# Weight decoding in five VectorE steps with range totals, spread over the first batch, more banks for early scratch, and a reordered prologue

## The chip, the core and the metric

The kernel runs on one core of a Trainium2 chip. The metric is the device time of one execution in microseconds (us). The engines of the core that matter here are TensorE (PE; its weight loads are listed apart as PEld), VectorE (DVE), ScalarE (ACT), GpSimd (POOL) and the queue that issues most transfers (SP). Each engine works through its own queue in order. What the measurement of this kernel can tell from no change is about 0.3%, some 4 us.

## The reference

Attention over clusters, and behind it a feed-forward block. For each of 4 batches and 8 heads there are 768 queries, keys and values of 64 numbers, and 16 centroids per head. Every query and key goes to the centroid whose direction is nearest, and a query sees only keys of its own cluster:

```
mask = q_assign[:, :, :, None] == k_assign[:, :, None, :]
scores = np.where(mask, scale * q @ k.T, -1e9)
attn = softmax(scores);  x = attn @ v      # (B*S, 512)
h = x @ w_in                               # 512 -> 2048
out = (h * clip(h + 3, 0, 6) / 6) @ w_out  # 2048 -> 512
```

The weights `w_in` and `w_out` arrive as 64-bit floats, 16.8 MB in all, and the engines cannot compute with these: they are loaded as pairs of 32-bit words (`lo`, `hi`) and decoded to 32-bit floats on the chip.

## The kernel before

`fast_path` does everything unless an input is out of range; a flag `ok` at the end chooses whether `general_path` is run afterwards (it never is here).

**Attention.** Heads are taken in 16 pairs, and a pair has 12 steps: 2 halves of the queries (`HALF` = 384) by 6 blocks of keys. A step (`scores`, then `attn_v` two steps later) is: TensorE makes the scores `ps`, ScalarE their exponent `ex` (L304), GpSimd adds `ex` to a running sum `acc` (L308 for the first sum of a half, L311 for the other four, five sums in each half), TensorE multiplies with the values (`pv`). Four steps after a half has ended `divide` sums `acc` over partitions on TensorE (`pd`, L342), and VectorE takes the reciprocal `rcp` (L346) and writes the quotient to `xT` (L347). The reciprocals are the clearest marks of progress in the trace: one per half, 8 in each batch of 4 pairs, 32 in all. I call the time from one reciprocal to the next "a half".

**Preparation of a pair.** While a pair runs, the next one is prepared: four groups of transposes (`turn`, tile `pqk`, copied to `xf` by VectorE and ScalarE in turn), the match with the centroids (`route`: `pr` on TensorE, then six VectorE instructions L248 to L264 up to the one-hot `oh`), and three groups of matmuls that turn `oh` round (`route_turn`, `po` to `xm`). All of these and `pd` share one PSUM buffer, the pool `psum_t` with one slot: the next group cannot be written before the copy of the last one has ended.

**Weights.** 32 chunks of 128x512 numbers, 16 of `w_in`, then 16 of `w_out`, 512 KB each. `load_weights` needs one of two `raw` buffers; `decode_chunk` has eight steps in a chain across two engines: VectorE cuts out exponent (L57) and fraction (L61), GpSimd clamps and shifts the exponent (L64, L67) and scales the fraction (L70), VectorE adds the low word (L73), multiplies (L76) and sets the sign (L77). By the source, 8 chunks are decoded in every 15 steps.

**Feed-forward.** When batch b has gone through `divide`, its feed-forward items go into a list `fill` and are put between the steps of batch b+1: `up` (`ph`, L368; ScalarE `t`, L375; VectorE `gT`, L377) and `down` (`py`, L390). They have the two slots of `psum_m`. While batch 0 runs there is nothing in `fill` and `psum_m` is empty. So the program has a first stage (prologue and batch 0, attention and decoding), a long second stage (three batches of attention with feed-forward work between), and the feed-forward work of the last batch by itself.

**What sets the order.** Within an engine the order is not the source's: a scheduler of the framework places each instruction by its own model of when its inputs and its buffer are ready. The queues as built are what counts, and the section on the change shows pieces of them.

**Range checks.** `divide` also folds `pd <= BOUND` into a tile `good` on VectorE (L352) and adds `rcp` to `inverses` on GpSimd (L355); at the end these give `ok`.

## Time and profile before

| what | value |
|---|---|
| device time, median of 3 runs | 1276.08 us (1273.18 to 1277.16) |
| the profiled execution | 1276.86 us |
| its span in the trace | 1274.5 us |
| busy: PE, DVE, POOL, ACT | 94%, 34%, 32%, 21% of the span |
| first `ex` starts | 30.88 us |
| first, seventh, eighth reciprocal start | 71.6, 216.0, 239.0 us |
| PE busy from 239 to 1122 us | 883.0 of 883.0 us |
| last copy of `y` starts | 1266.6 us |

The busy shares are means over stages that differ. Read by stretches, VectorE and GpSimd work most of the time up to some 240 us and little after it, TensorE has idle time up to there and none after it. The clock column (PEclk) gives the granted clock of TensorE as a share of the full 2.4 GHz.

### The profile page before, as it was taken

The page shows a single profiled execution, that of the slowest core. Times are in us where ns is not written, and L with a number is a line of the kernel's source. Part 1 is how long each engine was busy: PE and PEld are TensorE (multiplying, and loading weights), DVE is VectorE, ACT ScalarE, POOL GpSimd, SP SyncE. Part 2 cuts the span into 40 slices and gives each one's busy share as a digit, 9 for nine tenths or more (in the row PEclk, how much of TensorE's full clock was granted, in tenths as well). Part 3 has the DMA queues.
Part 4 walks back from the last instruction along what each step waited for, and adds up shares of the span by engine and source line. Part 5 has one row for each costly group of instructions (what it writes and reads, how often), then busy time and mean ns, then how long its engine had stood idle before and what let it go on. Part 6 is the DMA issues. An engine that isn't in the chain of part 4 may idle for free.

```text
span 1274.5 us, 11438 instructions
## 1 busy us (share of the span) xinstructions
PE 1196.9 (94%) x4610; PEld 546.9 (43%) x4610; DVE 439.0 (34%) x588; ACT 270.3 (21%) x403; POOL 409.5 (32%) x315
## 2 busy tenths in 40 slices
PE   5767777899999999999999999999999999999997
PEld 3323323445444454454434454454434444554553
DVE  5888778733213221232221322232212222120110
ACT  1222222232212320223112231123211321020110
POOL 2778677633232321233222322233322332000000
PEclk9788878799999999999999999999999999999999
DMA  5322332301010100201011010110110000000000
GB/s 141 91 85 85 103 91 79 104 1 38 5 46 12 25 13 9 54 1 38 1 30 33 13 25 9 29 25 15 23 30 9 1 1 8 17 1 16 9 9 20
DMA packets 83646, 42.81 MB, mean 34 GB/s; under 512 B 76416, under 2 KB 76416, under 8 KB 83584
## 3 DMA queue, kind: packets, MB, share of 16 engines
q1 hardware_dynamic: 83328, 41.95, 12.1%
q8 instruction: 38, 0.62, 0.2%
q14 instruction: 24, 0.20, 0.0%
q10 hardware_dynamic: 256, 0.03, 0.0%
HBM read 35.68 MB, written 6.29 MB: 33 GB/s over the span
## 4 chain that ended last, share of the span: by engine, by line
PE 82%; DVE 8%; POOL 6%; issue 2%; DMA 1%; ACTq 0%; ACT 0%; POOLq 0%
PE ph L368 27%; PE py L390 27%; PE ps L300 12%; PE pv L321 9%; DVE wfr L76 3%; PE pr L242 3%; POOL acc L311 2%; PE pqk L228 2%; POOL wex L64 1%; PE pd L342 1%; POOL wfr L70 1%; POOL wex L67 1%; PE po L276 1%; DVE wfr L73 1%; DVE rcp L346 1%
## 5 line engine op out<-in xcount | busy, mean ns | idle before, releaser
L368 PE MATMUL ph<-xT,w_in_sb 128*128 128x384 f32 x1024 | 359.3, 501 | 0.0
L311 POOL TENSOR_TENSOR acc<-acc,ex 128x768 f32<-128x768 f32 x128 | 241.0, 1883 | 327.5 <-ACT ex L304 325.9
L390 PE MATMUL py<-w_out_sb,gT 128*128 128x512 f32 x768 | 345.8, 602 | 0.0
L304 ACT ACTIVATE ex<-ps 128x768 f32<-128x768 f32 x192 | 155.7, 811 | 463.9 <-PE ps L300 455.4
L368 PEld LDWEIGHTS ph<-xT,w_in_sb 128*128 128x128 f32 x1024 | 190.9, 193 | 146.9 <-issue 25.3
L390 PEld LDWEIGHTS py<-w_out_sb,gT 128*128 128x128 f32 x768 | 142.8, 191 | 176.4 <-issue 175.8
L300 PE MATMUL ps<-xf 64*128 64x384 f32 x768 | 201.1, 569 | 0.0
L377 DVE SCALAR_TENSOR_TENSOR gT<-t,ph 128x384 f32<-128x384 f32 x128 | 70.8, 553 | 328.4 <-ACT t L375 328.3
L321 PE MATMUL pv<-ex,vt 128*64 128x384 f32 x768 | 176.9, 541 | 0.0
L375 ACT ACTIVATE t<-ph,half_c 128x384 f32<-128x384 f32 x128 | 74.4, 581 | 416.8 <-PE ph L368 416.8
L308 POOL TENSOR_TENSOR acc<-ex 128x768 f32<-128x768 f32 x32 | 58.8, 1839 | 234.4 <-ACT ex L304 234.0
L300 PEld LDWEIGHTS ps<-xf 64*128 64x128 f32 x768 | 66.1, 197 | 109.5 <-issue 99.8
L346 DVE RECIPROCAL rcp<-pd 128x384 f32<-128x384 f32 x32 | 81.8, 2555 | 72.6 <-PE pd L342 72.6
L396 DVE COPY y<-py 128x512 f32<-128x512 f32 x24 | 16.6, 692 | 195.8 <-PE py L390 195.8
L321 PEld LDWEIGHTS pv<-ex,vt 128*64 128x64 f32 x768 | 39.6, 140 | 95.4 <-issue 86.8
L300 PE MATMUL ps<-xm 64*128 64x384 bf16 x384 | 70.6, 341 | 0.0
L233 DVE COPY xf<-pqk 128x384 f32<-128x384 f32 x32 | 17.7, 555 | 107.9 <-PE pqk L228 107.9
L242 PEld LDWEIGHTS pr<-cnT,xf 128*128 128x128 f32 x384 | 46.5, 200 | 10.0 <-issue 7.2
L76 DVE TENSOR_TENSOR wfr<-wfr,wex 128x512 f32<-128x512 f32 x32 | 50.2, 1570 | 1.5 <-POOL wex L67 1.0
L242 PE MATMUL pr<-cnT,xf 128*128 128x32 f32 x384 | 48.4, 285 | 0.0
L355 POOL TENSOR_TENSOR inverses<-inverses,rcp 128x384 f32<-128x384 f32 x32 | 33.6, 1050 | 41.7 <-DVE rcp L346 41.7
L64 POOL TENSOR_SCALAR wex<-wex 128x512 int32<-128x512 int32 x32 | 25.2, 787 | 66.6 <-DVE wex L57 66.1
(61 smaller groups left out, 472.2 us busy)
## 6 DMA issues: line engine op xcount, KB each, us to landing
raw<-in_moe_w_in_dram SPq DMA_DIRECT2D x16, 512.0 KB, 3.7
raw<-in_moe_w_out_dram SPq DMA_DIRECT2D x16, 512.0 KB, 3.7
qk<-in_q_dram SPq DMA_DIRECT2D x32, 192.0 KB, 3.2
qk<-in_k_dram SPq DMA_DIRECT2D x32, 192.0 KB, 3.6
vt<-in_v_dram SPq DMA_DIRECT2D x32, 192.0 KB, 3.3
out_dram<-y SPq DMA_DIRECT2D x24, 256.0 KB, 2.0
cen<-in_centroids_dram ACTq DMA_DIRECT2D x8, 4.0 KB, 2.5
```

What stands on the lines that cost most here:

```text
L76: nc.vector.tensor_tensor(out=fr_f, in0=fr_f, in1=ex_f, op=ALU.mult)
L242: nc.tensor.matmul(pr[:, j], lhsT=xf[:, j], rhs=cnT[:, c0 : c0 + 2 * C], start=True, stop=True)
L300: nc.tensor.matmul(sc[:, t], lhsT=x[r, NCH + j], rhs=x[r, qs], start=first, stop=not first)
L304: nc.scalar.activation(out=ex, in_=sc, func=ACT.Exp, scale=SM_SCALE)
L308: nc.gpsimd.tensor_tensor(out=acc, in0=st["ex", n - 1], in1=ex, op=ALU.add)
L311: nc.gpsimd.tensor_tensor(out=acc, in0=acc, in1=ex, op=ALU.add)
L321: nc.tensor.matmul(pv[t * D : (t + 1) * D], lhsT=vt[:, j, t], rhs=ex[:, t], start=(j == 0), stop=(j == NCH - 1),)
L346: nc.vector.reciprocal(out=rcp, in_=pd)
L368: nc.tensor.matmul(hh, lhsT=w_in_sb[:, kt, f * P : (f + 1) * P], rhs=xT[:, kt, hf * HALF : (hf + 1) * HALF], start=(kt == 0), stop=(kt == ...
L375: nc.scalar.activation(out=t, in_=hh, func=ACT.Relu, bias=half_c, scale=1.0 / 6.0)
L377: nc.vector.scalar_tensor_tensor(out=gT, in0=t, scalar=1.0, in1=hh, op0=ALU.min, op1=ALU.mult)
L390: nc.tensor.matmul(py, lhsT=st["g", f][:, i * P : (i + 1) * P], rhs=w_out_sb[:, f], start=(f == 0), stop=(f == NFT - 1),)
```

## The change

Six things change.

- **Decoding.** The chain on two engines becomes five VectorE steps (L216, L220, L223, L227, L230 of the new file): shift the high word left by three, put its two top bits back, cut out the exponent (`unit`), scale the low word by it, add. Two ScalarE instructions for each chunk read the high words and add up a bound on the size (`Abs`, L207) and on what is too small (`Relu`, L210), with `accum_out`, for the flag at the end. GpSimd has no part in decoding any more.
- **Its place.** `chunks_by` gives 16 chunks to the 48 steps of batch 0 and the other 16 to the 13 steps after, by the source; the next chunk's load is issued ahead of a decoding and not behind it.
- **Range checks of `divide`.** L352 on VectorE and L355 on GpSimd go; two ScalarE copies with `accum_out` (L393) add up `pd` and `rcp` instead.
- **Banks.** While batch 0 runs, two of three scratch tiles (`pqk`, `pr`, `po`, `pd`) come from `psum_m`, so three banks and not one; behind it all come from `psum_t` as before.
- **Copies.** All three `xm` copies go to ScalarE (before: two on VectorE). One one-hot tile stands in place of two.
- **Prologue.** The four `turn` groups of pair 0 come before the centroid work and not after it, `v` is loaded after q and k, and a one-element `Exp` is put before the first real one.

The diff, cut to its core:

```diff
+    def scratch(shape, name):
+        st["scratch"] += 1
+        if st["early"] and st["scratch"] % 3:
+            return psum_m.tile(shape, F32, name=name, tag="m")
+        return psum_t.tile(shape, F32, name=name, tag="t")
...
     def decode_weights(i):
-        if 0 <= i < len(chunks):
-            decode_chunk(nc, decp, chunks[i][0], st.pop(("raw", i)))
+        dst, raw = chunks[i][0], st.pop(("raw", i))
+        lo, hi = raw[:, :, 0], raw[:, :, 1]
+        size = decp.tile([P, WC], BF16, name="wsize")
+        nc.scalar.activation(
+            out=size, in_=hi.bitcast(F32), func=ACT.Abs, accum_out=w_totals[:, 0, i : i + 1]
+        )
+        nc.scalar.activation(
+            out=size, in_=size, func=ACT.Relu, bias=w_low, scale=-1.0,
+            accum_out=w_totals[:, 1, i : i + 1],
+        )
+        nc.vector.tensor_scalar(
+            out=top, in0=hi, scalar1=3, scalar2=0x3FFFFFFF,
+            op0=ALU.logical_shift_left, op1=ALU.bitwise_and,
+        )
+        nc.vector.scalar_tensor_tensor(
+            out=top, in0=hi, scalar=0xC0000000, in1=top, op0=ALU.bitwise_and, op1=ALU.bitwise_or
+        )
+        nc.vector.tensor_scalar(
+            out=unit, in0=top, scalar1=0xFF800000, scalar2=None, op0=ALU.bitwise_and
+        )
+        nc.vector.scalar_tensor_tensor(
+            out=unit, in0=lo, scalar=2.0**-52, in1=unit, op0=ALU.mult, op1=ALU.mult
+        )
+        nc.vector.tensor_tensor(out=dst, in0=top, in1=unit, op=ALU.add)
...
-        nc.vector.scalar_tensor_tensor(
-            out=good, in0=pd, scalar=BOUND, in1=good, op0=ALU.is_le, op1=ALU.mult
-        )
-        nc.gpsimd.tensor_tensor(out=inverses, in0=inverses, in1=rcp, op=ALU.add)
+        for a, x in enumerate((pd, rcp)):
+            same = nump.tile([P, HALF], BF16, name="same", tag="same")
+            nc.scalar.activation(
+                out=same, in_=x, func=ACT.Copy, accum_out=totals[:, a, 2 * g + hf : 2 * g + hf + 1]
+            )
...
+    def chunks_by(n):
+        first = n * (NW // 2) // per_batch
+        return first if n <= per_batch else min(NW // 2 + (n - per_batch) * 5 // 4, NW)
...
-        for i in range(n * 8 // 15, (n + 1) * 8 // 15):
-            decode_weights(i - 1)
-            load_weights(i)
+        for i in range(chunks_by(n), chunks_by(n + 1)):
+            load_weights(i + 1)
+            decode_weights(i)
```

**VectorE in batch 0.** From the second reciprocal on, first of the kernel before, then of the changed one. `wex`, `wfr` and `wtop`, `wunit` are the tiles of a chunk being decoded, told apart by their numbers.

```order
L346 RECIPROCAL rcp_616<-pd_613 128x384
L352 SCALAR_TENSOR_TENSOR good_127<-pd_613,good_127 128x384
L347 TENSOR_TENSOR xT_471<-num_556,rcp_616 128x384
L73 SCALAR_TENSOR_TENSOR wfr_824<-raw_802,wfr_824 128x512
L57 TENSOR_SCALAR wex_870<-raw_833 128x512
L76 TENSOR_TENSOR wfr_824<-wfr_824,wex_823 128x512
L61 TENSOR_SCALAR wfr_871<-raw_833 128x512
L77 SCALAR_TENSOR_TENSOR w_in_sb_116<-raw_802,wfr_824 128x512
L248 TENSOR_REDUCE mx_679<-pr_666 128x24
L250 TENSOR_TENSOR tie_681<-pr_666,mx_679 128x384
L73 SCALAR_TENSOR_TENSOR wfr_871<-raw_833,wfr_871 128x512
```

```order
L386 RECIPROCAL rcp_593<-pd_590 128x384
L220 SCALAR_TENSOR_TENSOR wtop_1101<-raw_1035,wtop_1101 128x512
L387 TENSOR_TENSOR xT_470<-num_545,rcp_593 128x384
L223 TENSOR_SCALAR wunit_1102<-wtop_1101 128x512
L216 TENSOR_SCALAR wtop_1188<-raw_1096 128x512
L227 SCALAR_TENSOR_TENSOR wunit_1102<-raw_1035,wunit_1102 128x512
L220 SCALAR_TENSOR_TENSOR wtop_1188<-raw_1096,wtop_1188 128x512
L230 TENSOR_TENSOR w_in_sb_116<-wtop_1101,wunit_1102 128x512
L292 TENSOR_REDUCE mx_646<-pr_633 128x24
L223 TENSOR_SCALAR wunit_1189<-wtop_1188 128x512
L294 TENSOR_TENSOR tie_648<-pr_633,mx_646 128x384
```

Counted along the whole queue: before, 8 chunks are finished ahead of the first reciprocal, 3 in each of the next seven halves (29 ahead of the eighth) and 3 after it. Now 8 ahead of the first, 4 in each of the next six halves (32 ahead of the seventh), and none after it. So the queue as built has the whole decoding in batch 0, whatever `chunks_by` says of the 13 steps behind it.

**ScalarE in batch 0**, about the first half's end, before and after, with what each row waits for (`DMAHW` is a transfer).

```order
L304 ACTIVATE ex_550<-ps_545 128x768 [waits PE_49,Pool_49]
L327 COPY num_556<-pv_452 128x384 [waits PE_49]
L231 COPY xf_539<-pqk_570 128x384 [waits DVE_49,PE_49]
L304 ACTIVATE ex_580<-ps_575 128x768 [waits PE_49,Pool_49]
L304 ACTIVATE ex_608<-ps_603 128x768 [waits PE_49,Pool_49]
```

```order
L344 ACTIVATE ex_492<-ps_487 128x768 [waits PE_49,Pool_49]
L207 ACTIVATE wsize_921,w_totals_127<-raw_832 128x512 [waits DMAHW1_49]
L393 ACTIVATE same_477,totals_126<-pd_471 128x384 [waits DVE_49]
L393 ACTIVATE same_479,totals_126<-rcp_474 128x384
L210 ACTIVATE wsize_921,w_totals_127<-wsize_921,w_low_128 128x512 [waits Activation_49]
L344 ACTIVATE ex_502<-ps_497 128x768 [waits PE_49]
```

Between two exponents there now stand the size checks of a chunk, the first of them waiting for its transfer, and after a reciprocal the two totals.

**TensorE in the second stage**, from a `pd` that is followed by an `up` item, before and after (the second `pd` row of each).

```order
L342 MATMUL pd_1868<-acc_1616,ones_121 64x384
L368 MATMUL ph_1881<-xT_471,w_in_sb_116 128x384 x4
L300 MATMUL ps_1898<-xf_1415 128x384 [waits Activation_49]
L228 MATMUL pqk_1876<-ident_118,qk_1499 128x128 [waits DVE_49,PE_49]
L228 MATMUL pqk_1876<-ident_118,qk_1499 128x128 x2
L300 MATMUL ps_1898<-xf_1415 128x384
```

```order
L382 MATMUL pd_1885<-acc_1583,ones_121 64x384
L408 MATMUL ph_1900<-xT_470,w_in_sb_116 128x384 x4
L340 MATMUL ps_1917<-xf_1320 128x384 [waits Activation_49]
L340 MATMUL ps_1917<-xf_1320 128x384
L272 MATMUL pqk_1895<-ident_118,qk_1454 128x128 [waits PE_49,Activation_49]
L272 MATMUL pqk_1895<-ident_118,qk_1454 128x128 x2
```

The transposes behind `pd` waited for VectorE's last reading of `pd`; now they wait for ScalarE's, and both score matmuls stand ahead of them in place of one. There are 13 such places in the queue, and 8 more where `down` matmuls stand between. On ScalarE the total of `pd` stands behind the `t` of that same `up` item.

## Rows read from the trace of the kernel before

**Rows 1.** Stretches: us, busy PE, PEld, DVE, ACT, POOL (instructions), PEclk, DMA share, GB/s
```profile
31.00:72.00 41.00, 30.05 (x142) 12.46 (x142) 34.93 (x40) 10.65 (x15) 32.64 (x27) 0.82 0.29 84
...
192.00:216.00 24.00, 19.92 (x107) 8.58 (x103) 20.47 (x26) 6.71 (x10) 17.56 (x17) 0.82 0.29 77
216.00:239.00 23.00, 14.81 (x68) 5.61 (x67) 16.81 (x23) 4.95 (x7) 17.47 (x15) 0.84 0.38 100
239.00:1122.00 883.00, 883.00 (x3430) 403.17 (x3429) 236.01 (x319) 199.73 (x299) 243.06 (x150) 0.99 0.08 20
```

**Rows 2.** Tile rcp: ns shortest/median/longest, first and last start in us
```profile
L346 DVE RECIPROCAL rcp<-pd x32: 2544/2558/2559, 71.6 to 1080.9; 128x384 f32<-128x384 f32 x32
L355 POOL TENSOR_TENSOR inverses<-inverses,rcp x32: 992/995/1322, 74.2 to 1083.6; 128x384 f32<-128x384 f32 x32
L347 DVE TENSOR_TENSOR xT<-num,rcp x32: 549/1162/1649, 74.5 to 1083.8; 128x384 f32<-128x384 f32 x32
```

**Rows 3.** VectorE timeline, seventh and eighth reciprocal: start us, us, instruction
```profile
215.97 2.55 DVE L346 RECIPROCAL rcp<-pd 128x384 f32<-128x384 f32 x1
...
238.96 2.55 DVE L346 RECIPROCAL rcp<-pd 128x384 f32<-128x384 f32 x1
```

**Rows 4.** Tile wex, the same columns
```profile
L57 DVE TENSOR_SCALAR wex<-raw x32: 410/417/2034, 11.2 to 254.1; 128x512 uint32<-128x512 uint32 x32
L64 POOL TENSOR_SCALAR wex<-wex x32: 613/719/1119, 11.7 to 254.6; 128x512 int32<-128x512 int32 x32
...
L76 DVE TENSOR_TENSOR wfr<-wfr,wex x32: 672/1484/2298, 14.5 to 258.4; 128x512 f32<-128x512 f32 x32
```

**Rows 5.** Tile wfr, the same columns
```profile
L70 POOL TENSOR_SCALAR wfr<-wfr x32: 617/618/992, 12.5 to 256.1; 128x512 f32<-128x512 uint32 x32
L73 DVE SCALAR_TENSOR_TENSOR wfr<-raw,wfr x32: 684/692/1092, 13.1 to 257.7; 128x512 f32<-128x512 uint32 x32
```

**Rows 6.** Tile acc, the same columns
```profile
L311 POOL TENSOR_TENSOR acc<-acc,ex x128: 1798/1806/2326, 39.5 to 1071.9; 128x768 f32<-128x768 f32 x128
```

**Rows 7.** Timeline at 98 us, POOL and DVE side by side
```profile
98.14 2.31 POOL L311 TENSOR_TENSOR acc<-acc,ex 128x768 f32<-128x768 f32 x1
...
98.70 2.03 DVE L57 TENSOR_SCALAR wex<-raw 128x512 uint32<-128x512 uint32 x1
```

**Rows 8.** POOL sums from 30.8 to 71.6 us: busy us, mean ns, idle before
```profile
L311 POOL TENSOR_TENSOR acc<-acc,ex 128x768 f32<-128x768 f32 x7 | 14.5, 2078 | 0.3
...
L308 POOL TENSOR_TENSOR acc<-ex 128x768 f32<-128x768 f32 x2 | 4.0, 2004 | 0.1
```

**Rows 9.** DVE groups from 30 to 237 us, the same columns
```profile
L233 DVE COPY xf<-pqk 128x384 f32<-128x384 f32 x10 | 5.5, 549 | 0.3 <-PE pqk L228 0.3
...
L264 DVE TENSOR_TENSOR oh<-tie,first 128x192 bf16<-128x192 f32 x8 | 2.5, 348 | 0.0
L250 DVE TENSOR_TENSOR tie<-pr,mx 128x384 f32<-128x384 f32 x4 | 2.2, 554 | 0.1
```

**Rows 10.** Timeline of the prologue
```profile
10.94 0.29 DVE L215 COPY cnT<-pc 128x128 f32<-128x128 f32 x1 [0.63 <-PE pc L214]
...
18.82 5.33 PE L242 MATMUL pr<-cnT,xf 128*128 128x32 f32 x24
...
30.88 1.51 ACT L304 ACTIVATE ex<-ps 128x768 f32<-128x768 f32 x2
```

**Rows 11.** Timeline of a division in the second stage
```profile
303.22 2.85 PE L368 MATMUL ph<-xT,w_in_sb 128*128 128x384 f32 x8
303.34 2.56 DVE L346 RECIPROCAL rcp<-pd 128x384 f32<-128x384 f32 x1 [1.29 <-PE pd L342]
305.81 0.50 DVE L352 SCALAR_TENSOR_TENSOR good<-pd,good 128x384 f32<-128x384 f32 x1
...
306.11 0.58 ACT L375 ACTIVATE t<-ph,half_c 128x384 f32<-128x384 f32 x1 [3.35 <-PE ph L368]
...
306.84 0.55 PE L228 MATMUL pqk<-ident,qk 128*128 128x128 f32 x3
```

More of the change, by code (lines that the diff above doesn't have):

```diff
@@ L149, in fast_path @@
     cnT = const.tile([P, H * C], F32, name="cnT")
-    ohs = [const.tile([P, NC2, P], BF16, name=f"oh{i}") for i in range(2)]
-    good = const.tile([P, HALF], F32, name="good")
-    inverses = const.tile([P, HALF], F32, name="inverses")
-    st = {}
+    one_hot = const.tile([P, NC2, P], BF16, name="one_hot")
+    totals = const.tile([P, 2, NG], F32, name="totals")
+    w_totals = const.tile([P, 2, NW], F32, name="w_totals")
+    w_low = const.tile([P, 1], F32, name="w_low")
+    st = {"scratch": 0}
+    def scratch(shape, name):
[3 more added lines that the diff above has]
+        return psum_t.tile(shape, F32, name=name, tag="t")
     def load(g, *names):
@@ L276, in route_turn @@
             nc.tensor.matmul(
[L277 removed]
+                po[:, i], lhsT=one_hot[:, j], rhs=(ident_q if j < NCH else ident_k),
                 start=True, stop=True,
             )
[L280 to L284 removed]
+        nc.scalar.copy(out=xm[:, part * 4 : part * 4 + 4], in_=po)
     def where(n):
@@ L425, in fast_path @@
     total = NPAIR * per_pair
-    load(0, "q", "k", "v")
+    st["early"] = True
+    load(0, "q", "k")
     constants()
+    for part in range(4):
+        turn(0, part)
+    load(0, "v")
+    load(1, "q", "k")
     centroid_norm()
-    for step in prep_items(0).values():
-        step()
-    load(1, "q", "k")
+    route(0)
+    for part in range(3):
+        route_turn(0, part)
+    load_weights(0)
     lag_v, lag_d = 2, 4
```

54 lines of the change are left out of this document (33 added, 21 removed).

## The prediction

> **What bounds the kernel now.** I read the slices of the page first: VectorE and GpSimd are nearly full up to some 240 us and little used after it. Then the stretches between reciprocals [rows 1]: in a half of batch 0 (24.0 us from 192) TensorE is busy for 19.9 us at a granted clock of 0.82, and in the 23.0 us to the eighth reciprocal for 14.8 us; from 239 to 1122 us it is busy throughout at 0.99. So TensorE sets the second stage, and only the first can be shortened by work moved on other engines: the six halves from the first reciprocal at 71.6 [rows 2] to the seventh at 216.0 [rows 3] take 24.06 us each.
>
> What fills a half is seen in single instructions. A step that VectorE does in 0.41 us took up to 2.03, and one of 0.67 up to 2.30 [rows 4]; the timeline shows why: L57 starts at 98.70 behind a GpSimd sum that runs from 98.14 to 100.45, and ends at 100.73, with it [rows 7]. The two engines shut each other out. The reciprocal, which reads PSUM, is never longer than 2.56 us [rows 2], so it runs beside a sum. The Trainium skill says this as a rule (SBUF — State Buffer, section "SBUF: two separate sides"): VectorE in its two-port mode or with two SBUF inputs and GpSimd share a port pair as an exclusive lock held for a whole instruction. The trace agrees, with 2.03 against 0.41 us.
>
> I therefore add up what wants that port, at the shortest durations, in one half before: 3 chunks by 5 VectorE steps (two like L57 at 0.41, three from 0.67 to 0.69: 2.9 in all) [rows 4, 5] and 3 GpSimd steps (0.61 each, 1.85) [rows 4, 5], so 14.25; 5 sums at 1.80 [rows 6], 9.0; `inverses` 0.99 and `xT` 0.55 [rows 2]; half a `route` (0.55 for the step that reads `rank`, two of 0.35) [rows 9], 0.6. That is 25.4 against 24.06 measured, a factor of 0.947 (neighbours overlap a little at their ends). The port is full; that is the bound of batch 0.
>
> **The change, part by part.** The sum is made against the profiled execution: 1276.86 us, of which its span is 1274.5; it lies 0.8 above the median.
>
> *Prologue.* Before, `pr` starts at 18.82 and the first exponent at 30.88 [rows 10], since the four transposes wait for `cnT` (written by 11.2) and then share one bank. With the transposes done early and three banks, `pr` can follow `cnT`. But VectorE's queue now has three steps of chunk 0 ahead of the `cnT` copy (0.41 + 0.69 + 0.41 = 1.5) and four of chunk 1 between those of `route` (0.69 + 0.41 + 0.69 + 0.67 = 2.5), and ScalarE has one size check ahead of the first exponent (no row; priced as the 0.58 of `t` [rows 11], up to 1.5 if its load is late). So 5.8 us are won at `pr` (13.0 for 18.8) and 1.5 is already in that; 2.5 and 0.6 go again, leaving 2.4 (bounds 0 and 5): first exponent at 28.5.
>
> *First half, 40.7 us from there to the first reciprocal.* Port before: 6 chunks at 4.75, 9 sums [rows 8] at 1.80, a `route` 1.25, together 46.0, of which 40.7 is 0.886. Now 6 chunks at 2.9 (17.4), 16.2 and 1.25: 34.9, by that factor 30.9. That is the lower bound; TensorE's 30.05 busy us [rows 1] stand just under it. The upper one lets VectorE run its own work in series (17.4, a `route` of six steps 2.9, two `xf` copies at 0.55 [rows 9]: 21.4) and adds to each of 9 sums a full block of 1.63 (2.298 - 0.672 [rows 4]), 14.7: 36.1. I take 33, near the middle: first reciprocal at 61.5, so 10 earlier.
>
> *Six halves.* The queue holds 4 chunks in each, not 3, with a different mix. Removed: 3 GpSimd steps a chunk, `inverses` on GpSimd and `good` on VectorE. Port now: 4 x 2.9 = 11.6, sums 9.0, `xT` 0.55, 0.6: 21.75, by 0.947 20.6 us; the lower bound, which needs GpSimd always ready with a sum when VectorE does something else. The upper one, in series on VectorE: 11.6, reciprocal 2.55, `xT` 0.55, `xf` 0.55, half a `route` 1.45, together 16.7, and 5 blocks at 1.63: 24.9. One sum can run under the reciprocal, which makes it 23.2. GpSimd had work queued all the time before; with the sums alone it will often be waiting for an exponent when VectorE is off the port, so I go above the middle: 22.0. Six of them are 132, the seventh reciprocal starts at 193.5 and not at 216.0. With the first 10, that is 22.5.
>
> *Last half.* It had three chunks (23.0 us); now it has none. What is late next is TensorE, 14.8 us busy [rows 1]; the five sums are 9.0. I take 16 (bounds 14 and 19): 7 less, eighth reciprocal at 209.5, 29.5 earlier.
>
> *Three banks.* Costed at nothing by itself: it lets TensorE run ahead, but TensorE is not the bound of these halves. Without it the 16 us of the last half would not hold.
>
> *ScalarE in batch 0.* Per half it gets 4 x 2 size checks of 512 numbers and 2 totals of 384. No row has them with their running sum; by `t` with 384 numbers (0.58 [rows 11]) and an exponent with 768 (about 0.8 [rows 10]) they are 5.8 to 8 us, on top of 6.7 busy in 24.0 [rows 1]; 15 in 22 is not a bound. But the check waits for a transfer, and the exponents queue behind it; TensorE and GpSimd wait for these. Two `raw` buffers leave a load the time of one chunk (5.5 us at four in 22). Taken at nothing, since VectorE needs the same transfer; the upper bound is the second rival below. The skill speaks against this part (ScalarE: Activation LUTs, "Rules for kernel authors": give `relu`-like work to VectorE, not ScalarE). By it the checks would be two more port steps in each chunk, which in the sum above is what costs most; the trace speaks for ScalarE here.
>
> *Second stage.* The matmuls are the same, and so is the time that TensorE needs. Three chunks leave it, 8.7 us of VectorE work beside a TensorE that waits for nothing. One thing is new: the bank of `pd` is free when ScalarE has read it. Before: reciprocal and `good` end at 306.31 and the transposes start at 306.84, after one score matmul [rows 11]. Now ScalarE has `t` first (to 306.69), then the total (at most 0.58), so 307.2 or so: 0.4 later than TensorE gets there. Against that, both score matmuls now run as a pair ahead of the transposes. 13 places at 0.4 either way, so between 5 won and 5 lost; taken at 0. In the other 8 places `py` matmuls cover it. The end of the program has a few reductions more, all ahead of the last `y` but the two that were there.
>
> Sum: 1276.86 - 29.5 = **1247 us**.
>
> **The rivals.**
>
> *The port stays packed (first).* Halves of 20.6, first half 30.9, last half 14: the eighth reciprocal is at 28.5 + 30.9 + 123.6 + 14 = 197 us, 42 earlier, so 1235; with a prologue and a second stage at their good ends 1226. For it: before, the factor held to a few per cent in halves with and without `route`. Against it: GpSimd loses the backlog that made the packing good.
>
> *Every sum costs VectorE its full length, or the loads hold ScalarE (second).* Halves of 24.9, first half 36.1, last half 19: the eighth reciprocal at 28.5 + 36.1 + 149.4 + 19 = 233, 6 earlier: 1271; with the sum under the reciprocal 1260. For it: the steps of a chunk now all hang on each other on one engine, nothing comes between. Against it: no reciprocal in the trace was blocked.
>
> *Slower: ScalarE becomes the gate of the second stage.* The 24 divisions there free their bank through ScalarE's queue. If the total of `pd` comes behind an exponent (0.81 or less, half of the pair's 1.51 [rows 10]) besides `t`, TensorE stands for some 2 us at each: 24 x 2 = 48 lost, 29.5 won, 1295. It decides from 29.5 / 24 = 1.2 us a division. Against it: the queue as built has the total straight behind the `t` of the covering item, and 8 of the places lie under `py`.
>
> **How the numbers follow.** Forecast 0.52 (1240 to 1259), packed port 0.18 (1226 to 1240), full blocks 0.20 (1259 to 1276), ScalarE as gate 0.10. The time is that of the first, 1247. A range from 1230 to 1267 takes all of the first, most of the second and half of the third: 0.52 + 0.15 + 0.12, some 0.8. Faster by over 0.3% (under 1272.3, about what a measurement of this kernel can tell) are the first two and most of the third, 0.87; within it the end of the third and the start of the last, 0.06; slower 0.07.
>
> **What would show it.** First exponent near 28.5; reciprocals one, seven and eight near 61, 193 and 209; halves of 22 us with VectorE over 90% busy; GpSimd with nothing but sums; the last half near 16 us. From there 1035 us to the end, as before. Wrong would be: halves longer than 24 (sums that block more than once, or VectorE idle behind a load); a step of the new decoding much longer than 0.41 or 0.69 without a sum beside it; TensorE with gaps after 209 us, and ScalarE's totals as what ended them.

## The result, and the profile of the changed kernel

The changed kernel takes 1235.37 us (median of four runs, 1231.67 to 1240.62), the kernel before 1275.15 (1273.18 to 1277.16): a ratio of 0.9691, interval 0.9651 to 0.9731. The forecast was 1247, with a range from 1230 to 1267. The profiled execution took 1234.13 us, with a span of 1232.2. Against the profiled execution of before that is 42.7 us less (39.8 by the medians), of which 42.3 lie in the span and divide so:

| stretch | forecast | measured |
|---|---|---|
| start to first exponent | 28.5 | 29.63 |
| first reciprocal starts | 61.5 | 60.65 |
| six halves, to the seventh reciprocal | 6 x 22.0 | 136.9, so 22.8 each |
| last half of batch 0 | 16 (14 to 19) | 11.55 |
| eighth reciprocal starts | 209.5 | 209.11 |
| eighth to last (32nd) reciprocal | as before, 842.0 (within 5) | 827.57 |
| last reciprocal to end of span | as before, 193.6 | 195.5 |

So the first stage gave 29.9 us, as forecast to 0.4, but by luck: its four terms came out +1.1, -2.0, +4.9 and -4.5 us against the forecast, which cancel. The second stage, forecast at nothing, gave another 14.4, of which 2 went again at the end.

Stretches of the changed kernel between reciprocals (us, busy PE, PEld, DVE, ACT, POOL with instructions, PEclk, DMA share, GB/s), to be read against [rows 1]:

```profile
60.60:81.20 20.60, 17.20 (x93) 6.45 (x88) 20.36 (x25) 11.68 (x28) 9.66 (x5) 0.92 0.46 124
81.20:105.30 24.10, 17.53 (x85) 7.42 (x84) 23.96 (x30) 13.30 (x30) 10.26 (x5) 0.72 0.53 139
172.70:197.60 24.90, 19.98 (x118) 8.79 (x116) 24.64 (x32) 12.72 (x27) 11.72 (x6) 0.86 0.31 82
197.60:209.10 11.50, 8.55 (x50) 3.32 (x49) 4.09 (x5) 5.80 (x11) 5.86 (x4) 1.00 0.15 34
209.10:1036.70 827.60, 823.75 (x3320) 374.68 (x3321) 181.61 (x247) 230.14 (x410) 212.55 (x118) 1.00 0.08 20
```

With decoding in it, a half has VectorE at 99%, and GpSimd at 43 to 47% where it had 73% [rows 1]. Halves that prepare a pair by routing are longer (24.1, 24.9) than those that only transpose (20.6). The last half has no decoding, and VectorE has little to do there.

Tiles of VectorE in the changed kernel (ns shortest/median/longest, first and last start), answering to [rows 2] and [rows 4]; `wtop` from 60 to 210 us:

```profile
L386 DVE RECIPROCAL rcp<-pd x32: 2543/2557/2559, 60.7 to 1036.7; 128x384 f32<-128x384 f32 x32
L387 DVE TENSOR_TENSOR xT<-num,rcp x32: 540/558/2157, 63.7 to 1039.3; 128x384 f32<-128x384 f32 x32
...
L216 DVE TENSOR_SCALAR wtop<-raw x24: 409/418/2042, 60.3 to 187.5; 128x512 uint32<-128x512 uint32 x24
L220 DVE SCALAR_TENSOR_TENSOR wtop<-raw,wtop x24: 622/680/2297, 63.1 to 189.8; 128x512 uint32<-128x512 uint32 x24
```

The reciprocal is never held up; `xT`, for which `inverses` used to stand in the way, has a median of 558 ns where it had 1162; a step of the new decoding costs 0.42 or 0.68 in most cases, and up to 2.30. The timeline has the reason, as in [rows 7]: a step that starts during a sum ends just behind it (here at 102.10, the sum at 101.54).

```profile
99.72 1.82 POOL L351 TENSOR_TENSOR acc<-acc,ex 128x768 f32<-128x768 f32 x1 [5.26 <-ACT ex L344]
99.92 2.18 DVE L227 SCALAR_TENSOR_TENSOR wunit<-raw,wunit 128x512 f32<-128x512 uint32 x1
```

The first of these two rows also shows what is new: GpSimd stood for 5.26 us before the sum, waiting for an exponent. From 60 to 210 us these waits are 82.7 us in 31 places.

### The profile page after: what moved, and what is told of

Read it like the earlier page. It is cut to its first block, busy times and chain, and to the rows that moved or that the text cites. A ratio compares the mean times of both kernels' runs of the same rounds, so it can differ in the third digit from the quotient of the medians.

```text
span 1232.2 us, 11493 instructions
## 1 busy us (share of the span) xinstructions
PE 1167.3 (95%) x4610; PEld 537.4 (44%) x4610; DVE 392.2 (32%) x527; ACT 362.3 (29%) x693; POOL 296.4 (24%) x186
## 3 DMA queue, kind: packets, MB, share of 16 engines
q1 hardware_dynamic: 83328, 41.95, 12.9%
## 4 chain that ended last, share of the span: by engine, by line
PE 83%; DVE 13%; ACT 1%; DMA 1%; issue 1%; SPq 0%; POOL 0%; ACTq 0%; POOLq 0%
PE ph L408 28%; PE py L430 27%; PE ps L340 11%; PE pv L361 9%; PE pr L286 3%; DVE wunit L227 3%; DVE wtop L220 2%; PE pqk L272 2%; DVE wunit L223 2%; DVE wtop L216 1%; DVE rcp L386 1%; PE pd L382 1%; DVE w_out_sb L230 1%; DVE w_in_sb L230 1%; PE po L320 1%
## 5 line engine op out<-in xcount | busy, mean ns | idle before, releaser
L408 PE MATMUL ph<-xT,w_in_sb 128*128 128x384 f32 x1024 | 352.1, 493 | 0.0
L351 POOL TENSOR_TENSOR acc<-acc,ex 128x768 f32<-128x768 f32 x128 | 235.5, 1840 | 441.3 <-ACT ex L344 440.9
L408 PEld LDWEIGHTS ph<-xT,w_in_sb 128*128 128x128 f32 x1024 | 187.3, 190 | 142.2 <-issue 17.1
L340 PE MATMUL ps<-xf 64*128 64x384 f32 x768 | 188.2, 560 | 12.3 <-ACT ex L344 11.7
L361 PE MATMUL pv<-ex,vt 128*64 128x384 f32 x768 | 172.9, 530 | 9.9 <-ACT num L367 9.9
L340 PEld LDWEIGHTS ps<-xf 64*128 64x128 f32 x768 | 61.2, 192 | 114.6 <-issue 91.3
L361 PEld LDWEIGHTS pv<-ex,vt 128*64 128x64 f32 x768 | 39.3, 139 | 103.1 <-issue 80.2
L340 PE MATMUL ps<-xm 64*128 64x384 bf16 x384 | 66.4, 337 | 0.0
L277 DVE COPY xf<-pqk 128x384 f32<-128x384 f32 x32 | 17.8, 555 | 115.1 <-PE pqk L272 115.1
L272 PE MATMUL pqk<-ident,qk 128*128 128x128 f32 x192 | 37.6, 311 | 10.4 <-DMA qk<-in_q_dram 5.2
L272 PEld LDWEIGHTS pqk<-ident,qk 128*128 128x128 f32 x192 | 22.1, 151 | 47.1 <-issue 28.8
L207 ACT ACTIVATE wsize<-raw 128x512 bf16<-128x512 f32 x32 | 21.6, 676 | 51.5 <-DMA raw<-in_moe_w_out_dram 28.1
```

Of the source, the lines that this page charges most:

```text
L272: nc.tensor.transpose(out=pt[:, i], in_=qk[:, j // NCH, j % NCH], identity=ident)
L340: nc.tensor.matmul(sc[:, t], lhsT=x[r, NCH + j], rhs=x[r, qs], start=first, stop=not first)
L351: nc.gpsimd.tensor_tensor(out=acc, in0=acc, in1=ex, op=ALU.add)
L361: nc.tensor.matmul(pv[t * D : (t + 1) * D], lhsT=vt[:, j, t], rhs=ex[:, t], start=(j == 0), stop=(j == NCH - 1),)
L408: nc.tensor.matmul(hh, lhsT=w_in_sb[:, kt, f * P : (f + 1) * P], rhs=xT[:, kt, hf * HALF : (hf + 1) * HALF], start=(kt == 0), stop=(kt == ...
```

## The experiments

The durations of halves below come from the starts of the reciprocals in each kernel's trace. "Chunks" are counted by the last step of the new decoding in the stretch (L230, or its like), or by the multiplication of the old (L76).

### Is the shared port the bound?

**The sums left out.** In `scores`:

```
-        elif j > 1:
+        elif j > 1 and g >= NKT:
```

> The changed kernel with GpSimd's sums of batch 0 left out, but for the first of each half (the divisors there are then too small, and the computation is left incomplete). Theory of the port: what makes a step of VectorE longer is a sum; without them VectorE works its own 16.7 us of a half in series, with at most one block of 1.63: halves of 17 to 18.5 us for 22.8, TensorE's own 13 to 17 just under it. Eighth reciprocal 30 to 36 earlier, and hardly a step of the decoding over 0.45 or 0.72. Rival (VectorE waits for transfers, or its queue for ScalarE and TensorE): halves of 21 us or more, so under 12 us won.

Measured: 1194.69 us (one run). The six halves took 103.4 us, 17.2 each, and the eighth reciprocal came at 169.8, 39.3 earlier. The decoding from 55 to 170 us, same columns:

```profile
L220 DVE SCALAR_TENSOR_TENSOR wtop<-raw,wtop x24: 626/680/694, 57.2 to 155.1; 128x512 uint32<-128x512 uint32 x24
...
L216 DVE TENSOR_SCALAR wtop<-raw x23: 411/420/1823, 58.6 to 154.2; 128x512 uint32<-128x512 uint32 x23
```

Of 24 instructions L220 none is longer than 0.694 us now, where they went up to 2.297; the odd long one among L216 stands beside the one sum of a half that is left. From the first to the seventh reciprocal, the changed kernel and then this run:

```profile
60.65:197.56 136.91, 104.77 (x543) 42.33 (x538) 135.04 (x159) 76.03 (x173) 60.94 (x31) 0.83 0.42 115
54.76:158.18 103.42, 86.98 (x524) 37.21 (x522) 97.96 (x160) 77.38 (x179) 11.87 (x6) 0.98 0.55 151
```

The same work of VectorE takes 37.1 us less, so each of the 24 sums that are gone had cost it 1.55 us, not much under the prediction's full block of 1.63. What remains of a half is VectorE's own work in series, 16.7 by the prediction. The four sums, on another engine, cost 5.6 us of each half: that is shown.

**The old decoding put back.** `decode_weights` calls the `decode_chunk` of before.

```
-        lo, hi = raw[:, :, 0], raw[:, :, 1]
...
-        nc.vector.tensor_tensor(out=dst, in0=top, in1=unit, op=ALU.add)
+        decode_chunk(nc, decp, chunks[i][0], st.pop(("raw", i)))
...
-        nc.scalar.activation(out=w_totals[:, 0, 0:1], in_=w_low, func=ACT.Exp)
```

> The changed kernel with one part undone: a chunk is decoded by the steps of before, three of them on GpSimd (the totals of the weights' sizes on ScalarE, part of the range check, are left out). Theory of the port: a chunk wants 4.75 us of it and not 2.9. First half with 8 chunks (38.0 + 16.2 + 1.25) x 0.886 = 49, six halves with 3.5 chunks each (16.6 + 9.0 + 0.55 + 0.6) x 0.947 = 25.3, last half 12 to 14: eighth reciprocal at 29 + 49 + 152 + 13 = 243, so 34 later than with the new steps, some 1269. Rival (the gain came from the totals, the banks and the order, and the steps of the decoding hardly matter, since what leaves GpSimd comes on ScalarE): within 8 us of 1235.

Measured: 1269.15 us (ten runs, 1261.73 to 1273.64), 0.9947 of before (0.9924 to 0.9971). First and eighth reciprocal at 62.9 and 239.1, six halves of 25.5. With banks, totals and prologue new (but for the one-element `Exp`, which is out here) and the old steps, the eighth reciprocal stands where it stood before: without the decoding nothing of the first stage's gain is left.

**ScalarE's size checks left out.**

```
-        nc.scalar.activation(
-            out=size, in_=hi.bitcast(F32), func=ACT.Abs, accum_out=w_totals[:, 0, i : i + 1]
-        )
...
-            accum_out=w_totals[:, 1, i : i + 1],
-        )
...
-        nc.scalar.activation(out=w_totals[:, 0, 0:1], in_=w_low, func=ACT.Exp)
```

> The changed kernel without the size checks of the weights on ScalarE (part of the range check is left out). Theory of the port: they do not touch what sets the halves: from the first to the seventh reciprocal 137 us within 2, 1235. Rival (a check waits for its transfer, the exponents queue behind it, and GpSimd and TensorE wait for these): halves shorter by 1 us each or more, 1229 or less.

Measured: 1238.64 us (1237.48 to 1239.78), no shorter than with them; six halves 136.5 us for 136.9. The first exponent came 1.5 us earlier (28.12), the eighth reciprocal 1.0 (208.1). ScalarE does wait for transfers at these checks in the changed kernel, 41.3 us from 60 to 210 us, but that isn't what ends last there.

These and the later runs give one table. "Port" is the prediction's sum for a half (2.9 or 4.75 a chunk, sums 9.0, `xT` 0.55, routing 0.6, `inverses` 0.99 where it exists):

| kernel | chunks in six halves | port, us a half | measured | quotient |
|---|---|---|---|---|
| before | 18 | 25.4 | 24.06 | 0.95 |
| changed, old decoding | 21 | 26.8 | 25.5 | 0.95 |
| before, totals alone | 19 | 25.2 | 24.5 | 0.97 |
| changed, no size checks | 25 | 22.2 | 22.8 | 1.02 |
| changed, one bank | 21 | 20.3 | 21.0 | 1.04 |
| changed | 24 | 21.75 | 22.8 | 1.05 |
| before, new decoding alone | 21 | 21.3 | 23.1 | 1.09 |

With GpSimd's three decoding steps in it a half is 3 to 5% shorter than the sum, without them 2 to 5% longer. Only the last row needs something more.

### The parts alone

**The new decoding in the kernel before** (with one one-hot tile, to make room).

```
-            decode_chunk(nc, decp, chunks[i][0], st.pop(("raw", i)))
+        lo, hi = raw[:, :, 0], raw[:, :, 1]
...
+        nc.vector.tensor_tensor(out=dst, in0=top, in1=unit, op=ALU.add)
```

> The kernel before with one part of the change alone: the new five steps of a chunk with their totals on ScalarE (to make room for the tile of totals there is one one-hot tile, as in the changed kernel). Theory of the port: a half with three chunks wants 8.7 + 9.0 + 0.99 + 0.55 + 0.6 = 19.8 us of it, x 0.947 = 18.8, and in series on VectorE 13.8 with five blocks of 1.63 22.0; between them 20.5, against 24.06. Six halves 21 us less, the first half 6 to 8 less, the last half 1 to 3 less: 28 to 32 won, 1243 to 1248. Rival (one bank holds TensorE, whose matmuls take 17 to 20 us of a half): halves not under 22.5, so 10 to 15 won, 1260 to 1266. Rival (the second stage's gain of 14.4 us came with the totals, or with the chunks that left it): here the time from the eighth to the last reciprocal stays at 842, as before.

Measured: 1256.47 us, 0.9846 of before (0.9809 to 0.9883): 18 us and not 28 to 32. The eighth reciprocal came 15.4 earlier (223.6). The queue came out with 21 chunks in the six halves and not the 18 that the expectation reckoned with; but the halves are also 9% longer than the port's sum for 21, so the port alone fails here, and the rival with one bank is nearer. Halves that transpose took 20.5, those with a routing 23.0, 27.1 and 27.1. TensorE's waits, then VectorE's, from 68 to 207 us (us in total, times, longest):

```profile
PE po L306 <- DVE good L382: 13.0, 3, 4.4
PE pqk L258 <- DVE good L382: 6.0, 3, 2.6
DVE mx L278 <- PE pr L272: 6.0, 2, 3.0
DVE xm L314 <- PE po L306: 5.8, 3, 2.3
```

`good` is the last reader of `pd` in the single bank and stands in VectorE's queue behind decoding; `po` waits for that bank, and VectorE for `pr` and `po`. So VectorE isn't full here: it is busy for 122.6 of 138.7 us. In the run with one bank in the changed kernel, below, which has the same 21 chunks, it is busy for 121.4 of 126.1. What makes the difference, `good` and two of three `xm` copies on VectorE, `inverses` on GpSimd or the old prologue, is not told apart.

The last rival was about the second stage: it took 838.5 us for 842.0, and its halves of 30.15 us stayed as they were.

**The totals alone in the kernel before.**

```
-            out=good, in0=pd, scalar=BOUND, in1=good, op0=ALU.is_le, op1=ALU.mult
-        )
-        nc.gpsimd.tensor_tensor(out=inverses, in0=inverses, in1=rcp, op=ALU.add)
+        for a, x in enumerate((pd, rcp)):
+            same = nump.tile([P, HALF], BF16, name="same", tag="same")
+            nc.scalar.activation(
...
```

> The kernel before with one other part alone: the two range totals of a division on ScalarE, in place of good on VectorE and inverses on GpSimd (and a single one-hot tile, as in the changed kernel). Theory: in the second stage the bank of pd comes free behind ScalarE and the score matmuls go ahead of the transposes as a pair; the halves of 30.15 there become 29.77, and 12 or 13 like them lose 0.36 each: 4.5 us, and the time from the eighth to the last reciprocal falls by that, dips of the clock aside. In the first stage 0.99 of port work less in a half, by 0.947, seven times: 6.6 us. In all 11 us: 1263. Rival (the 0.36 belongs to the copies of xm, which the change gives to ScalarE alone, or to the decoding): the halves stay at 30.15, 1268. Rival (ScalarE holds TensorE at the divisions): 1280 or more.

Measured: 1272.42 us (ten runs), 0.9981 of before (0.9958 to 1.0004): no difference that the runs can tell. Its two parts went in opposite ways. In the second stage, as expected, the halves of 30.15 us became 29.77. In the first stage 6.6 us were to be won, and the eighth reciprocal came 4.5 later (243.45). Of TensorE's waits the largest, here from 60 to 244 us and in the kernel before from 60 to 240:

```profile
PE po L272 <- ACT same L350: 23.0, 4, 7.3
PE po L276 <- DVE good L352: 15.2, 4, 5.9
```

In one bank `po` waits for ScalarE's total now, where it waited for `good`. But all waits of TensorE together are 47.4 us in both traces, so that this cost anything is not shown. What differs is the queue: ahead of the eighth reciprocal 31 chunks are through L76 and not 29. At 0.95 of 4.75 us the two are 9.0 us by estimate, 2.4 more than the 6.6 won; the other 2 are open.

**One bank in the changed kernel.**

```
-        if st["early"] and st["scratch"] % 3:
+        if False:
```

> The changed kernel with one part undone: the small PSUM tiles of the first batch all come from the one bank of psum_t again, as before. Theory (the port that VectorE and GpSimd share sets the halves of batch 0): the six halves from the first to the seventh reciprocal stay at 22.8 us within 0.5, since TensorE isn't the bound there; what changes is the first exponent, later by 1 to 3 us, and the last half, without decoding, 15 to 16 us for 11.55, since there TensorE is the bound and one bank makes it wait. Eighth reciprocal 5 to 8 later, some 1242. Rival (the banks let TensorE run ahead, and this is what made the halves shorter): the halves go back by 1 us or more each, so 11 us or more in all, 1247 or more.

Measured: 1244.19 us (1243.21 to 1245.5). The eighth reciprocal came at 213.7. The halves did not stay at 22.8; they took 21.0, since with one bank the queue came out with other numbers of chunks: 9 before the first reciprocal (67.5), 21 in the six halves, 2 in the last (20.16 us). Per chunk the port's price holds (table), so the rival falls too. TensorE's waits from 67 to 214 us show whom the bank waits for:

```profile
PE pqk L272 <- DVE xf L277: 11.6, 3, 4.0
PE po L320 <- ACT same L393: 8.4, 4, 4.9
```

**One bank, with the fifth to eighth half free of decoding** (the edit above, on the kernel of the next section).

> The changed kernel with w_out decoded behind the gT items, and the small PSUM tiles of the first batch in one bank again. The fifth to eighth half have no decoding in either, so that they show the banks by themselves: with three banks 15.40, 13.23, 16.99 and 13.23 us, 58.9 in all. Theory (without VectorE's decoding TensorE bounds a half, and one bank makes it stand between its small tiles): 3 to 5 us more in each, so 71 to 79. Rival (the banks matter only while VectorE is full): within 1 us each.

Measured: these halves took 17.80, 14.01, 16.21 and 14.01, so 62.0 us for 58.9 (one run, 1221.44 in all). My theory falls: where VectorE is free, one bank costs 0.8 us a half. The waits for a bank from 110 to 187 us are 3.6 us. The kernel as a whole takes 10.5 us more than with three banks (1210.94, next section), and 7.4 of these are there at the first reciprocal (67.9 for 60.5), with nine chunks ahead of it and not eight. So the banks are worth something while VectorE decodes, in part by what the queue comes out as, and little where it doesn't.

### From the cause to a faster kernel

If the port sets batch 0 and TensorE the rest, decoding belongs where VectorE is idle. `w_out` is not needed before the `py` items of batch 1.

**The 16 chunks of `w_out` behind the `gT` of the first 16 `up` items.**

```
+                if b == 0 and hf == 0:
+                    with tc.issue_after(ins.ins):
+                        load_weights(NW // 2 + f + 1)
+                        decode_weights(NW // 2 + f)
...
-        for i in range(chunks_by(n), chunks_by(n + 1)):
+        for i in range(chunks_by(n), min(chunks_by(n + 1), NW // 2)):
```

> The changed kernel with the sixteen chunks of w_out loaded and decoded behind the gT of the first sixteen up items, in the first half of the second batch, where VectorE is little used; they are needed only by the py matmuls of that batch. Theory of the port: 46 us of VectorE's work leaves the first stage. With 16 chunks left (w_in alone), the halves with no or few chunks fall to TensorE's bound of some 12 to 17 us; the eighth reciprocal comes 25 us earlier, at 184, and the second stage loses nothing, since VectorE has room: 1210. Rival (the decode's steps come ahead of reciprocal, routing and gT on VectorE's queue and hold TensorE in the second batch): the halves of that batch get longer by 3 us and more, and half or more of the gain goes: 1222 or more.

Measured: 1210.94 us, 0.9497 of before (0.9464 to 0.9531). Stretches, columns as above:

```profile
117.00:132.40 15.40, 15.40 (x102) 7.40 (x102) 7.46 (x9) 7.80 (x14) 9.10 (x6) 1.00 0.24 53
132.40:145.60 13.20, 13.20 (x78) 5.01 (x77) 5.55 (x4) 7.31 (x13) 9.01 (x6) 1.00 0.14 32
...
210.00:242.30 32.30, 29.93 (x123) 13.74 (x123) 27.34 (x41) 18.05 (x43) 10.19 (x5) 0.95 0.37 110
```

A half without decoding is TensorE's: busy 100% of 13.2 or 15.4 us at the full granted clock (17.0 at 0.90 in the seventh), where it had been given 0.72 to 0.92 while it stood and went. The eighth reciprocal came at 175.8, 8 us earlier than expected; but the ninth to eleventh half, where nothing was to be lost, were 6.3 us longer than in the changed kernel (TensorE 29.93 busy of 32.30 in the tenth). That the total is the 1210 of the expectation is luck.

**`w_in` spread as well.** 6 chunks early, then 1, 2, 1, 2, 1, 2, 1 behind the divisions:

```
+    def decode_paced(i, ins):
+        with tc.issue_after(ins.ins):
+            load_weights(i + 1)
+            decode_weights(i)
...
+            for i in (range(6 + 3 * hd // 2, 6 + 3 * (hd + 1) // 2) if hd < 7 else ()):
+                decode_paced(i, divided)
```

> The changed kernel with w_out decoded behind the gT of the first sixteen up items, as before, and w_in spread: two chunks ahead of the first routing's end, four behind it, and then one or two behind each division, as many as find room in the port beside TensorE's work. Theory of the port: a half with one chunk wants (2.9 + 10.15) x 1.05 = 13.7, one with two and a routing (5.8 + 10.75) x 1.05 = 17.4; TensorE wants 13.2 and 15.4 to 17.0. First reciprocal at 57 to 60, eighth at 58 + 4 x 13.6 + 3 x 17.0 = 163, so 12 earlier than with w_in decoded as early as it can be (175.8); the second stage as there: 1198 to 1202. Rival (when the chunks are decoded hardly matters, as long as VectorE's work in the stage is the same): within 3 us of 1211. Rival (a chunk behind each division comes ahead of the routing's steps and holds TensorE): 1206 or more, with TensorE waiting for one_hot.

Measured: 1243.16 us (1241.56 to 1244.18), 32 us worse than without this step, and halves of 20 to 21.7 us, of which VectorE is busy for 10 to 14. ScalarE's timeline in one of them:

```profile
90.31 0.81 ACT L349 ACTIVATE ex<-ps 128x768 f32<-128x768 f32 x1 [3.56 <-PE ps L345]
95.58 0.66 ACT L207 ACTIVATE wsize<-raw 128x512 bf16<-128x512 f32 x1 [4.46 <-DMA raw<-in_moe_w_in_dram]
...
96.24 0.79 ACT L349 ACTIVATE ex<-ps 128x768 f32<-128x768 f32 x1
96.93 0.47 ACT L372 COPY num<-pv 128x384 f32<-128x384 f32 x1
```

A size check waits 4.46 us for its transfer; behind it in the queue stand an exponent and `num`, and TensorE's next `pv` waits for `num` (23.6 us in five places from 25 to 230 us; for `one_hot`, which the expectation's last rival named, 10.9 in four). It is the mechanism of the prediction's second rival, "the loads hold ScalarE"; in the changed kernel it is hidden behind a full VectorE, here it decides.

**A third `raw` buffer, loads two chunks ahead** (and one buffer each for the decoding's own tiles).

```
-    rawp = pool("rawp", 2)
-    decp = pool("decp", 2)
+    rawp = pool("rawp", 3)
+    decp = pool("decp", 1)
...
-            load_weights(i + 1)
+            load_weights(i + 2)
```

> The paced kernel (w_in spread over the halves, w_out behind the gT items) with three raw buffers and the loads two chunks ahead, so that a load has landed when ScalarE's size check comes up (one buffer each for the decoding's own tiles makes the room). Theory (what the paced kernel lost came from late loads: ScalarE waited up to 6.7 us at a size check, with the copy num and the exponents queued behind it): those waits go, the halves fall from 20 to 13.5 to 17, the eighth reciprocal comes at 163 to 170 for 205.8, and the total is 1198 to 1208. Rival (the chunks behind each division hold VectorE when routing and TensorE need it): the halves stay at 19 us or more, 1230 or more.

Measured: 1233.87 us; the waits at the check were 57 us in all where they had been 55, and the halves stayed at 18.5 to 21.3. The loads still came late; SP's queue from 60 to 210 us shows why:

```profile
SPq L199 <- DVE wunit L227: 92.9, 11, 16.0
SPq L186 <- PE pqk L277: 43.3, 4, 11.3
```

SP waits for a buffer of `raw`, or for TensorE to free the one `qk` tile, and all loads stand in one queue behind that. The rival's number came true, its cause only in part: from 25 to 230 us TensorE waits 19.2 us for `num` and 15.5 for `one_hot`.

**The paced loads on ScalarE's queue**, behind a division's totals, with the size check behind the next division's.

```
+            with tc.issue_after(totaled.ins):
+                for i in (range(6 + 3 * (hd + 1) // 2, 6 + 3 * (hd + 2) // 2) if hd < 7 else ()):
+                    load_weights(i, nc.scalar)
```

> The paced kernel once more (w_in spread over the halves, w_out behind the gT items, three raw buffers), with the paced loads taken off SP's queue, where they stood behind the loads of q and k that wait for TensorE's transposes: they are issued behind a division's totals on ScalarE's queue, half a pair before they are decoded, and their size check stands behind the next division's totals. Theory (late loads at the size check were what held ScalarE, and behind it num, the exponents and TensorE): ScalarE's waits for transfers go, from 57 us to under 10; halves of 13.5 to 17.5, the eighth reciprocal at 163 to 172, in all 1198 to 1210. Rival (a chunk behind each division holds VectorE when routing needs it, and TensorE waits for one_hot): halves of 18 or more, 1222 or more.

Measured: 1208.17 us (1205.38 to 1211.57). ScalarE's waits at the check fell from 57 us to 20, not under 10. The halves that transpose took 12.93, as the first theory has it; those with a routing 21.5 to 22.1, as the rival has it. What was waited for, TensorE and then VectorE, from 25 to 230 us:

```profile
PE po L326 <- DVE one_hot L314: 19.0, 4, 5.8
...
DVE rcp L392 <- PE pd L388: 35.8, 8, 6.4
```

Both theories are right in half of the halves: two chunks ahead of a routing hold TensorE for it, and then VectorE stands before the reciprocal.

**The second chunk of such a half behind the routing.**

```
             items[r]()
+            if st["routed"] is not st.get("late") and 1 <= g < 4:
+                decode_paced(5 + 3 * g, st["routed"])
```

> The paced kernel with the loads on ScalarE's queue, and in each half with a routing the second chunk moved from behind the division to behind the routing's one_hot, ahead of the next reciprocal. Theory (in these halves TensorE stood 5.8 us for one_hot, since VectorE had two chunks ahead of the routing, while later VectorE stood 4.5 us for pd): the routing halves go from 21.5 to 16.5 to 18.5, the others stay at 12.9 to 13.5; eighth reciprocal at 163 to 168 for 177.0, in all 1194 to 1200. Rival (the port decides over both halves of a pair, wherever the chunk lies): the pair keeps its 34.4 us within 1.5, so 1204 to 1209.

Measured: **1195.26 us** (five runs, 1192.89 to 1199.43), 0.9367 of before (0.9349 to 0.9385). Two neighbouring halves:

```profile
71.90:89.70 17.80, 15.46 (x101) 7.40 (x102) 17.08 (x18) 10.72 (x22) 9.94 (x6) 1.00 0.30 75
89.70:102.70 13.00, 13.00 (x78) 5.14 (x79) 9.79 (x10) 8.55 (x17) 9.10 (x6) 1.00 0.38 112
```

All seven halves are 12.9 or 17.8 us, the eighth reciprocal comes at 164.2, and this kernel is 40 us faster than the changed one with the same instructions of arithmetic. Where they stand is worth as much as the change. (The rival's pair of 34.4 us is 30.7.)

## Why the prediction was right, and where it was not

**The bound.** Right. The port was taken for full, and taking the sums away, or putting the old decoding back, moves the halves the way that the sum of port work says, to 17.2 and 25.5 for 22.8; without the sums VectorE's own work in series is nearly all of a half (97.96 of 103.42 us). The Trainium skill's rule (SBUF — State Buffer, section "SBUF: two separate sides") agrees with the trace here too: L216 took 0.409 us alone and up to 2.042 beside a sum.

**Prologue and first half.** 28.5 and 61.5 forecast, 29.63 and 60.65 measured; the first exponent won 1.25 and not 2.4, the first half took 31.0 and not 33, near its packed lower bound of 30.9. `pr` started at 15.67 and not at 13.0: the copy to `cnT`, at 14.21, stood behind three decoding steps as reckoned, and TensorE then had two score matmuls first. The one-element `Exp` gave nothing: its table was loaded at 5.68, another at 7.20 for `cennrm`, and a third load of 1.28 us stands ahead of the first exponent at 28.33, as it did before at 29.59.

**Six halves.** The step "GpSimd loses the backlog, so I go above the middle" was right in kind: the quotient went from 0.95 to 1.05. It was sized 0.8 us short in each half, 4.9 in all. Nearer was the upper bound with one sum under the reciprocal, 23.2: each of the four sums costs VectorE 1.55 us by the run without them. The two ends of the range, 20.6 and 24.9, turn out to be nearly the two kinds of half: about 21.3 with transposes only, 24.4 with a routing. The 3.1 between them are about the 2.9 that the prediction counts for a routing on VectorE, which is full in both.

**Last half.** Mis-sized: 11.55 for 16, outside its bounds of 14 to 19. The step that failed is "14.8 us busy [rows 1]" as TensorE's need. That was at a granted clock of 0.84; at 1.00 such a half is 13.2 (fifth to eighth half of the run with `w_out` later), and TensorE had done part of it in the half before: 8.55 us are left in it (50 matmul records, where that run has 78). "Without the banks the 16 us would not hold" was wrong: with one bank and no decoding such a half took 14.0.

**ScalarE in batch 0.** Costed at nothing, rightly (136.5 for 136.9 without the checks), but for the wrong reason in part: it does stand 41 us at transfers. The cover was VectorE's full queue; where that was thinned, the same wait cost over 20 us (1233.9 to 1208.2 with the loads on another queue). The Trainium skill's advice against such work on ScalarE (ScalarE: Activation LUTs, "Rules for kernel authors") would have put the checks on the one engine that was full; the run without them shows that on ScalarE they cost no time here.

**Second stage.** This is the step that failed: taken at 0, between 5 won and 5 lost, and 14.4 us were won. Three terms, by the lengths of the halves in the two traces:

- The halves that were 0.36 to 0.38 shorter, 13 with those that also lost something else: 4.8 us. That is the prediction's 13 places at 0.4, whose sign it left open: the good end. The totals alone reproduce it (30.15 to 29.77), so it is the totals that do it. Both of its terms are there (rows below): TensorE waits 0.30 us for ScalarE's total, and the scores as a pair win more than that.
- Five halves (9th, 11th, 19th, 21st, 29th) that are 1.7 us shorter still: 8.6 us. In the trace of before their granted clock is 0.95 (0.91 in the ninth), in the changed kernel's 1.00.
- Another 1.0 us in the ninth, whose first 11 us had a clock of 0.87 before, just behind a stage in which TensorE stood and went.

TensorE's scores behind a division, before (from the first to the start of `pv` 2.32 us; the transposes at 306.84 are in [rows 11]) and in the changed kernel (1.96):

```profile
306.00 0.91 PE L300 MATMUL ps<-xf 64*128 64x384 f32 x2
...
308.32 0.54 PE L321 MATMUL pv<-ex,vt 128*64 128x384 f32 x2
```

```profile
273.01 0.92 PE L340 MATMUL ps<-xf 64*128 64x384 f32 x4
274.22 0.55 PE L272 MATMUL pqk<-ident,qk 128*128 128x128 f32 x3 [0.30 <-ACT same L393]
274.70 0.34 PE L340 MATMUL ps<-xm 64*128 64x384 bf16 x2
274.97 0.54 PE L361 MATMUL pv<-ex,vt 128*64 128x384 f32 x2
```

Stretches of before (the ninth half's start, and a dip in the 11th), then PE rows of that dip, and the same place in the changed kernel:

```profile
239.00:250.00 11.00, 11.00 (x44) 5.19 (x42) 7.88 (x11) 3.17 (x5) 7.65 (x8) 0.87 0.48 121
...
314.00:318.00 4.00, 4.00 (x27) 3.27 (x27) 1.33 (x3) 0.00 (x0) 1.77 (x1) 0.86 0.00 0
318.00:322.00 4.00, 4.00 (x14) 1.90 (x14) 1.95 (x5) 0.58 (x1) 0.00 (x0) 0.71 0.00 0
```

```profile
313.70 2.87 PE L242 MATMUL pr<-cnT,xf 128*128 128x32 f32 x24
316.40 4.52 PE L368 MATMUL ph<-xT,w_in_sb 128*128 128x384 f32 x8
```

```profile
280.34 2.87 PE L286 MATMUL pr<-cnT,xf 128*128 128x32 f32 x24
283.05 2.83 PE L408 MATMUL ph<-xT,w_in_sb 128*128 128x384 f32 x8
```

Behind the same 24 small matmuls the same eight took 4.52 us in one trace and 2.83 in the other. These dips don't belong to the change: in the 21st half the changed kernel's trace has 34.93 us, three others with its second stage (one bank, `w_out` later, no size checks) 36.62 or 36.63; the ninth takes 33.2 at a clock of 0.95 without the size checks; and the changed kernel with the old decoding has no dip at all there; its profiled execution is also the fastest of its ten (1261.73 us, median 1269.15). Each of the traces has between none and five. What sets off a dip is open. That the profile of before had five and that of the changed kernel none is some 9 of the 42.7 us between the two profiles.

**The rivals.** "The port stays packed" named 1235, which is the time that came, but by luck; its mechanism did not come: halves of 20.6 and the eighth reciprocal at 197 were not there. "Full blocks" at 24.9 missed the halves; with one sum under the reciprocal, 23.2, its mechanism is the one that the run without sums bears out. ScalarE as the gate of the second stage: TensorE is busy for 823.75 of 827.60 us there, so no. The gaps that were to be a sign of it are there, ended by ScalarE's totals, but small (us in total, times, longest; all of TensorE's waits from 209 to 1040 us):

```profile
PE pqk L272 <- ACT same L393: 2.1, 7, 0.3
PE po L320 <- ACT same L393: 1.8, 6, 0.3
```

Open: at the end of the program the span runs 9.8 us past the start of the last copy of `y`, where it ran 7.9. The work there is the same but for a few reductions ahead of it; no run was made for it. From the issue of the last store to the end it is 9.1 us for 7.2, and 7.0 in the last kernel, which has the same reductions, so these don't decide it.

## What to carry to other kernels

Where two engines share a port, add up what both want of it at the shortest durations, and compare with the stage: the quotient (0.95 to 0.97 in three kernels with decoding on both engines, 1.02 to 1.05 in three without) told the halves to some 5%, but 1.09 where VectorE stood waiting for TensorE. Count the work of a stage in the trace: the queue as built had more than once other numbers of chunks in it than the expectation. The cheapest gain is then to move such work to a stage in which another engine is the bound. Check what stands in front of the moved work in every queue, loads included: the same decoding in other places took 1243, 1234, 1208 and 1195 us. Before a difference between two single profiles is explained, take out the stretches where the granted clock differs.

## What the runs showed of the hardware

A ScalarE instruction with a running total is two instructions. Tile `wsize` of the changed kernel:

```profile
L207 ACT ACTIVATE wsize<-raw x32: 655/673/710, 12.3 to 187.6; 128x512 bf16<-128x512 f32 x32
L207 ACT ACTIVATION_READ_ACCUMULATOR wsize<-raw x32: 185/188/235, 12.9 to 188.2; 128x1 f32 x32
```

The second costs 0.19 us each time, so a chunk's two checks take 1.77 us and not the 1.4 of the two main instructions; ScalarE had the room.

In the halves of batch 0 in the changed kernel, where TensorE had gaps, the granted clock was 0.72 to 0.92. Gaps alone don't tell it: in the last kernel it was 1.00 in halves without a gap, but also in those of 17.80 us with 15.46 busy, and the dips above came in stretches without any. TensorE's need, estimated from a stretch with a low clock, is too high, as with the 14.8 us above that were 13.2.
